# A two-part kernel on one core: PSUM banks taken oldest first in the projection stage, loop tiles laid over inputs, output weights loaded last from SyncE, twelve copies moved to ScalarE

## Chip, cores, metric

One core of one Trainium2 chip. The metric is the device time of one execution in microseconds (us), the median of several; lower is better. A single profiled execution of each kernel gives the traces; its span (first to last instruction) is about 1.8 us shorter than its time.

In this kernel TensorE writes its products to banks of the memory PSUM; VectorE or ScalarE copies them out to SBUF, from where TensorE reads its operands; SyncE and ScalarE issue the transfers (DMA) between SBUF and DRAM. In the profile lines, SPq and ACTq are such issues by SyncE and ScalarE, with the time that the issue itself took. A DMA share of 1.0 or a little above means that the 16 DMA engines were full.

## The reference, cut to what matters

`x` is 2048 x 512. The result is a gated mix of two attention branches over the same `x`.

```python
g = _sigmoid((x * gate_w).sum(-1, keepdims=True))
a = _A_ref(x, ...)      # 64 segments of 32 rows, 32 heads of 128; 8 memory rows go from segment to segment
b = _B_ref(x, ...)      # 32 heads of 16, 4 blocks of 512 rows; a state of phi(k) v goes from block to block
return g * a + (1 - g) * b

# in A, for each segment (strictly one after the other):
h = jnp.concatenate([mem, xs], axis=1)
q, k, v = h @ Wq, h @ Wk, h @ Wv        # 512 -> 32 x 128
p = _softmax(q k^T, masked)
o = jnp.einsum('bhte,hed->btd', p v, Wo)
mem = o[:, :M, :]                       # the next segment needs this
# in B: phi = lambda t: jnp.where(t > 0, t + 1.0, jnp.exp(t)), for keys and queries
```

The kernel runs B's projections (keys, queries, values, phi) first, as a **first stage** of some 70 us, and stores them to DRAM. Then the **loop** over A's 64 segments (13.3 us each) takes up B's attention beside it, reading those tensors back. While the first stage runs, A's weights (Wk, Wq, Wv, Wo, 4.19 MB each) are loaded.

## The kernel before: the parts concerned

```python
class Banks:                                  # the eight PSUM banks
    def take(self, long=False):
        f = self.free                         # in the order in which they were given back
        if long:
            c = [b for b in f if b < 2] or f
        else:                                 # spare the whole pairs, if there are few
            whole = [b for b in f if b > 1 and b ^ 1 in f]
            c = [b for b in f if b not in whole and b > 1] if len(whole) <= 4 else [b for b in f if b > 1]
            c = c or [b for b in f if b > 1] or f
        b = c[0]
        f.remove(b)
        return b

# two layouts of the same stretch of SBUF: one for the first stage, one for the loop
in_p = alloc(esP, ("wkB", ...), ("wqB", ...), ("phK", ...), ("MZ16", ...), ...          # inputs
      ("etmp", [128, 512], BF16, 5), ("stgp", [128, 512], BF16, 3), ("stgk", [128, 512], BF16, 4), ("stgq", [128, 512], BF16, 4),
      ("V17", [128, 4, HB, 17], BF16, 0), ("wvB", [128, C, DM], BF16, 0))               # stg*, V17: staging of the stores
esP.close()
v.x_sb = v.Wo_sb[:, 0:NTT, :]                 # x lies in the first half of Wo's memory
in_a = alloc(esA, ("xL", ...), ("LN_sb", ...), ("KTL", ..., 2), ("QTL", ..., 2), ("VL", ..., 2), ("KN_sb", ...), ("QN_sb", ...),
      ("KT_sb", ...), ("QT_sb", [128, H // 2, L, 2], BF16, 0), ("V_sb", ...), ...)      # QT_sb falls on stgp

# the first stage, piece by piece
for n in range(len(pieces)):
    ...                                       # x chunks, gates
    pieces[n]()                               # a projection, its copy out of PSUM, its store from SyncE
    if n in (50, 52, 54, 56):
        bat.load(0, n // 2 % 2, "kv"[n // 54])          # the first blocks of B read back
    if weights and n % 4 == 2 and n > 5:
        weights.pop(0)()                      # one load of 1 MB from ScalarE: Wk x4, Wq x4, Wv x4, Wo x4
while weights:
    weights.pop(0)()                          # the rest, and B's output weights
plan_a(v, NSEG_RUN)                           # the loop

# one quarter of Wo, from ScalarE's queue; a single semaphore group for all four
P.dma(grp, lambda s: s.dma_start(v.Wo_sb[:, 8 * q:8 * q + 8, :], wosrc[:, 8 * q:8 * q + 8, :]),
      writes=[Rs("Wo")] + [...], name="dma_Wo%d" % q, eng="act")

# copies out of PSUM in the first stage
v.evac("dve" if m == "k" else "act", stage[:, :], v.pb[bk], ...)                        # keys, queries
v.evac("act" if tt % 2 else "dve", v.V17[:, tt, :, 0:16], v.pb[bk]...)                  # values
```

The softmax here doesn't subtract the row's maximum and nothing guards it: scores larger than these inputs give would overflow.

## Time and profile before

| | before |
|---|---|
| time, median of 3 | 947.72 us (946.32 to 948.25) |
| span of the profiled run | 946.2 us |
| segment 1 of the loop begins (its first projection of `hT`) | 99.86 us |
| from there to the end | 846.3 us |

TensorE's timeline of the kernel before in the first stage (start, busy time, engine, line, operation, tiles, shapes, count, and in brackets the idle time before and what ended it):

```profile
13.46 0.81 PE L634 MATMUL ps<-xT,wqB 128*128 128x512 bf16 x3 [0.79 <-DVE stgk L357]
16.81 1.04 PE L634 MATMUL ps<-xT,wqB 128*128 128x512 bf16 x4 [0.56 <-DVE stgk L357]
...
28.39 0.81 PE L634 MATMUL ps<-xT,wqB 128*128 128x512 bf16 x3 [1.47 <-DVE xT L357]
```

A projection (in two of the twelve cases below a transpose) waits for the copy that empties the bank it is to write: the bank rule gives out one emptied a moment ago. There are twelve such waits from 10 to 60 us, 8.6 us together.

ScalarE's queue at the end of the stage, where Wo is issued:

```profile
64.76 0.39 ACTq L502 DMA_DIRECT2D Wo_sb<-in_A_Wo_dram  x1
68.27 0.41 ACTq L502 DMA_DIRECT2D Wo_sb<-in_A_Wo_dram  x1
70.91 4.01 ACTq L502 DMA_DIRECT2D Wo_sb<-in_A_Wo_dram  x2
```

The issue of one 1 MB load normally takes 0.4 us of the queue. The last pair takes 4.01 us: when its second issue began, at about 71.3 us, three loads were outstanding (the first of them landed at 73.7), and the queue held ScalarE up until 74.9. The last quarter of Wo landed at 87.5 us.

### The profile page before, as it was taken

Reading aid. Unit: us, or ns where it says so; the run is one execution under the profiler, and the core shown is the slowest. Engines: PE = TensorE matmul, PEld = TensorE weight load, DVE = VectorE, ACT = ScalarE, POOL = GpSimd, SP = SyncE. Lnnn points to the kernel's source line nnn. Section 1 sums busy time; section 2 is a strip of 40 time slices with the busy share of each in tenths; the row PEclk is TensorE's granted clock in tenths of the full one; section 3 lists DMA queues with packets and bytes.
Section 4 is the critical chain, followed back from the end, with each engine's and each line's share of the span. In section 5 each row is a group of like instructions: output and inputs, shape, how many; then the busy total and the mean of one; then the engine's idle time right before and its main releaser. Section 6 shows DMA issues by size and latency. Waiting matters only on the chain. (4 is left out here: it accounts for less than half of the span.)

```text
span 946.2 us, 51712 instructions
## 1 busy us (share of the span) xinstructions
PE 875.4 (93%) x23175; PEld 466.7 (49%) x23182; DVE 635.1 (67%) x1388; ACT 575.4 (61%) x1339; POOL 243.6 (26%) x553
## 2 busy tenths in 40 slices
PE   8886989999899999999999989999999999999885
PEld 3443545555454545555455545545455555544442
DVE  4763666676666786776776777667767677677564
ACT  3542666666666766666666665666666666664553
POOL 3610222222222231322222232222222232221110
PEclk9997999999999999999999999999999999999999
DMA  9997000000001121101001110100101110000110
GB/s 305 371 343 247 13 13 16 15 21 18 22 9 38 32 54 28 27 16 27 16 21 49 32 44 20 28 15 19 41 16 41 31 43 24 24 3 9 37 37 8
DMA packets 66052, 51.36 MB, mean 54 GB/s; under 512 B 34464, under 2 KB 64296, under 8 KB 64296
## 3 DMA queue, kind: packets, MB, share of 16 engines
q1 hardware_dynamic: 59944, 31.29, 12.1%
q10 hardware_dynamic: 5888, 16.78, 5.0%
q8 instruction: 182, 2.98, 1.3%
q14 instruction: 38, 0.31, 0.1%
HBM read 33.47 MB, written 14.57 MB: 51 GB/s over the span
## 5 line engine op out<-in xcount | busy, mean ns | idle before, releaser
L801 ACT ACTIVATE PT<-ps 128x1024 bf16<-128x1024 f32 x160 | 163.8, 1024 | 1.8
L947 PE MATMUL ps<-Wv_sb,hT 128*32 128x512 bf16 x2048 | 143.5, 385 | 0.0
L947 PE MATMUL ps<-Wq_sb,hT 128*32 128x512 bf16 x2048 | 134.5, 380 | 0.0
L947 PE MATMUL ps<-Wk_sb,hT 128*32 128x512 bf16 x2048 | 132.7, 379 | 0.0
L808 POOL TENSOR_SCALAR_AFFINE_SELECT PT<-PT 128x512 bf16<-128x512 bf16 (+1 forms) x96 | 75.8, 789 | 199.9 <-ACT PT L801 175.3
L1000 PE MATMUL ps<-Wo_sb,OT_sb 128*32 128x512 bf16 x2048 | 123.4, 380 | 0.3 <-DVE OT_sb L357 0.2
L357 DVE CAST V_sb<-ps 128x512 bf16<-128x512 f32 x128 | 88.5, 691 | 47.7 <-PE ps L947 47.7
L1218 POOL TENSOR_TENSOR P_sb<-P_sb,R_sb 128x64 bf16<-128x64 bf16 x128 | 47.4, 371 | 280.0 <-PE ps L1172 166.7
L959 DVE STREAM_TRANSPOSE QT_sb<-QN_sb 128x256 f32<-128x256 f32 x128 | 56.7, 443 | 77.9 <-ACT QN_sb L355 70.1
L355 ACT ACTIVATE QN_sb<-ps 128x512 bf16<-128x512 f32 x128 | 77.1, 602 | 31.3 <-PE ps L947 28.8
L355 ACT ACTIVATE OT_sb<-ps 128x320 bf16<-128x320 f32 x128 | 56.0, 437 | 61.9 <-PE ps L1241 59.7
L1011 DVE TENSOR_TENSOR WL<-ps,WH 128x256 bf16<-128x256 f32 x128 | 54.3, 424 | 46.0 <-ACT WH L355 42.5
L1181 ACT ACTIVATE P_sb<-ps 128x224 bf16<-128x224 f32 x128 | 45.2, 353 | 60.8 <-PE ps L1172 60.8
L947 PEld LDWEIGHTS ps<-Wk_sb,hT 128*32 128x32 bf16 x2048 | 54.0, 97 | 48.7 <-ACT KN_sb L355 1.2
L357 DVE CAST OT_sb<-ps 128x320 bf16<-128x320 f32 x128 | 61.8, 483 | 20.3 <-PE ps L1241 18.9
L947 PEld LDWEIGHTS ps<-Wq_sb,hT 128*32 128x32 bf16 x2048 | 49.7, 96 | 44.6 <-ACT hT L355 9.3
L959 DVE STREAM_TRANSPOSE KT_sb<-KN_sb 128x256 f32<-128x256 f32 x128 | 56.5, 441 | 21.3 <-ACT KN_sb L355 19.1
L1000 PEld LDWEIGHTS ps<-Wo_sb,OT_sb 128*32 128x32 bf16 x2048 | 48.1, 96 | 45.1 <-DVE OT_sb L357 5.5
L787 PE MATMUL ps<-QTj,KTj 32*128 32x256 bf16 (+1 forms) x768 | 62.9, 255 | 4.3 <-ACT PT L801 3.6
L355 ACT ACTIVATE WH<-ps 128x256 bf16<-128x256 f32 x64 | 24.6, 384 | 62.6 <-PE ps L1000 59.7
L1205 ACT ACTIVATE R_sb<-ps 128x160 f32<-128x160 f32 x128 | 39.1, 305 | 35.8 <-PE ps L1198 35.8
L1228 PE MATMUL ps<-P_sb,V_sb 32*128 32x40 bf16 x2048 | 36.3, 178 | 22.2 <-ACT OT_sb L355 7.7
(131 smaller groups left out, 1578.5 us busy)
## 6 DMA issues: line engine op xcount, KB each, us to landing
Wk_sb<-in_A_Wk_dram ACTq DMA_DIRECT2D x4, 1024.0 KB, 6.9
Wq_sb<-in_A_Wq_dram ACTq DMA_DIRECT2D x4, 1024.0 KB, 8.2
Wv_sb<-in_A_Wv_dram ACTq DMA_DIRECT2D x4, 1024.0 KB, 7.8
Wo_sb<-in_A_Wo_dram ACTq DMA_DIRECT2D x4, 1024.0 KB, 10.9
scr_vd<-V SPq DMA_DIRECT2D x16, 136.0 KB, 6.3
Vj<-scr_vd SPq DMA_DIRECT2D x32, 68.0 KB, 2.5
Wo_sb<-in_A_x_dram SPq DMA_DIRECT2D x8, 256.0 KB, 6.1
scr_kTd<-stgk SPq DMA_DIRECT2D x16, 128.0 KB, 8.0
```

Source lines behind the costliest of these rows:

```text
L355: P.op("act", lambda a: a.activation(dst, src, ACT.Copy), reads=[v.rbank[k] for k in bks], writes=dres, name=name)
L357: P.op("dve", lambda d: d.tensor_copy(dst, src), reads=[v.rbank[k] for k in bks], writes=dres, name=name)
L787: ins = pe.matmul(v.pb[bks[x]][:, 256 * e + o:256 * e + o + w], KT[e][r, 128 * kc:128 * (kc + 1)], QT[r, q0:q0 + w], start=True, stop=True ...
L801: P.op("act", lambda a: a.activation(pt[:, :, :], v.ps[:, bks[0]:bks[1] + 1, :], ACT.Exp, scale=v.SCALE_B), reads=[v.rbank[b] for b in bks ...
L808: P.op("gp", lambda g: g.affine_select(mv, mv, [[0, mv.shape[1]], [1, 128]], ALU.is_ge, 0.0, base=0, channel_multiplier=-1), reads=[rp], w ...
L947: ins = pe.matmul(pb[bk][SEG * j:SEG * (j + 1), :], lhs(c), cols(w, j) if split else w[:, 512 * j:512 * (j + 1)], start=(c == 0), stop=(c ...
L959: P.op("dve", lambda d: d.transpose(to, src), reads=reads, writes=writes, name=name)
L1000: ins = pe.matmul(pb[bk][SEG * j:SEG * (j + 1), :], lhs(4 * k + j), Wo_sb[:, 4 * k + j, :], start=(first and k == ks[0]), stop=False, skip ...
L1011: P.op("dve", lambda d: d.tensor_tensor(lo[:, c], pb[bk][:, c], hi[:, c], ALU.subtract), reads=[rbank[bk], Rs(res[0][hf])], writes=[Rs(res ...
L1181: P.op("act", lambda a: a.activation(P_sb[:, b, :], pb[bk][:, 0:224], ACT.Exp, scale=SCALE), reads=[rbank[bk]], writes=[Rs("P%d" % b), Rs( ...
L1205: P.op("act", lambda a: a.activation(R_sb[:, b, :], pb[bk][:, 224:384], ACT.Ln), reads=[rbank[bk]], writes=[Rs("R%d" % b)], name="ln%d_%d" ...
L1218: P.op(ENG["n"], lambda d: d.tensor_tensor(left(P_sb), left(P_sb), grp04(R_sb[:, b, :]), ALU.mult), reads=[Rs("R%d" % b)], writes=[Rs("P%d ...
```

## The change

The intent: TensorE shall not wait for banks in the first stage (oldest bank first; twelve copies from the busier VectorE to ScalarE). The loop's first tiles shall not wait for the last stores (they are laid over inputs, which engines have finished reading, not over staging buffers that stores still read). ScalarE's queue shall not be held up at the end of the stage (Wo is issued by SyncE after all stores; B's output weights only in segment 1). For that, the A weights start earlier (n = 2, not 6), and so do the first blocks read back (n = 36 to 42, not 50 to 56).

The tile lists are cut to their names here.

```diff
 class Banks:
+        self.oldest = True
...
+        elif self.oldest:
+            c = [b for b in f if b > 1] or f
...
-    in_p = alloc(... wkB, wqB, phK, MZ16, bmask, mem0_sb, gwr_sb, beta_sb, gB_sb, omgB_sb, etmp x5, stgp x3, stgk x4, stgq x4, V17, wvB)
+    in_p = alloc(... wkB, wqB, phK, etmp x5, bmask, mem0_sb, gwr_sb, beta_sb, gB_sb, omgB_sb, wvB, MZ16, stgk x4, stgq x4, V17, stgp x3)
-    in_a = alloc(... xL, LN_sb, KTL x2, QTL x2, VL x2, KN_sb, QN_sb, KT_sb, QT_sb, ...)
+    in_a = alloc(... xL, LN_sb, KTL0, QTL0, VL0, KN_sb, QN_sb, KT_sb, QT_sb, ..., KTL1, QTL1, VL1, ...)
...
-        if n in (50, 52, 54, 56):
-            bat.load(0, n // 2 % 2, "kv"[n // 54])
-        if weights and n % 4 == 2 and n > 5:
+        if n in (36, 38, 40, 42):
+            bat.load(0, n // 2 % 2, "kv"[n // 40])
+        if weights and n % 4 == 2:
             weights.pop(0)()
-    while weights:
-        weights.pop(0)()
+    v.wo_load()                                   # the four Wo loads, one after the other, from SyncE
+    v.BK.oldest = False
+    v.BK.free = sorted(v.BK.free)
     plan_a(v, NSEG_RUN)
...
-        v.evac("dve" if m == "k" else "act", stage[:, :], ...)
+        v.evac("dve" if m == "k" and f < 3 else "act", stage[:, :], ...)
-        v.evac("act" if tt % 2 else "dve", v.V17[:, tt, :, 0:16], ...)
+        v.evac("act", v.V17[:, tt, :, 0:16], ...)
...
+        if s == 1:
+            v.wob_load()                          # B's output weights, in segment 1
```

More of the change, by code (lines that the diff above doesn't have):

```diff
@@ L282, in build @@
     esP = ExitStack()
-    in_p = alloc(esP, ("wkB", [128, C, DM], BF16, 0), ("wqB", [128, C, DM], BF16, 0), ("phK", [128, 4, DM], BF16, 0), ("MZ16", [128, 544], BF16, 0),
+    in_p = alloc(esP, ("wkB", [128, C, DM], BF16, 0), ("wqB", [128, C, DM], BF16, 0), ("phK", [128, 4, DM], BF16, 0), ("etmp", [128, 512], BF16, 5),
           ("bmask", [128, 136], BF16, 0), ("mem0_sb", [128, DM], BF16, 0), ("gwr_sb", [128, 128], BF16, 0), ("beta_sb", [128, HB], BF16, 0),
-          ("gB_sb", [128, HB], F32, 0), ("omgB_sb", [128, HB], F32, 0),
-          ("etmp", [128, 512], BF16, 5), ("stgp", [128, 512], BF16, 3), ("stgk", [128, 512], BF16, 4), ("stgq", [128, 512], BF16, 4),
-          ("V17", [128, 4, HB, 17], BF16, 0), ("wvB", [128, C, DM], BF16, 0))
+          ("gB_sb", [128, HB], F32, 0), ("omgB_sb", [128, HB], F32, 0), ("wvB", [128, C, DM], BF16, 0), ("MZ16", [128, 544], BF16, 0),
+          ("stgk", [128, 512], BF16, 4), ("stgq", [128, 512], BF16, 4), ("V17", [128, 4, HB, 17], BF16, 0), ("stgp", [128, 512], BF16, 3))
     esP.close()
@@ L291, in build @@
     esA = ExitStack()
-    in_a = alloc(esA, ("xL", [128, C, SEG], BF16, 0), ("LN_sb", [128, 2, 512], BF16, 0), ("KTL", [128, H // 2, SEG, 2], BF16, 2), ("QTL", [128, H // 2, SEG, 2], BF16, 2),
-          ("VL", [128, 2, 512], BF16, 2), ("KN_sb", [128, 2, 512], BF16, 0), ("QN_sb", [128, 2, 512], BF16, 0),
-          ("KT_sb", [128, H // 2, SEG, 2], BF16, 0), ("QT_sb", [128, H // 2, L, 2], BF16, 0), ("V_sb", [128, 2, 512], BF16, 0),
-          ("P_sb", [128, 2, 224], BF16, 0), ("R_sb", [128, 2, 160], F32, 0),
-          ("OT_sb", [128, H, L], BF16, 0), ("OTL", [128, H, SEG], BF16, 2),
+    LT = [128, H // 2, SEG, 2]
+    in_a = alloc(esA, ("xL", [128, C, SEG], BF16, 0), ("LN_sb", [128, 2, 512], BF16, 0), ("KTL0", LT, BF16, 0), ("QTL0", LT, BF16, 0), ("VL0", [128, 2, 512], BF16, 0),
+          ("KN_sb", [128, 2, 512], BF16, 0), ("QN_sb", [128, 2, 512], BF16, 0), ("KT_sb", LT, BF16, 0), ("QT_sb", [128, H // 2, L, 2], BF16, 0),
+          ("V_sb", [128, 2, 512], BF16, 0), ("P_sb", [128, 2, 224], BF16, 0), ("R_sb", [128, 2, 160], F32, 0),
+          ("OT_sb", [128, H, L], BF16, 0), ("OTL", [128, H, SEG], BF16, 2), ("KTL1", LT, BF16, 0), ("QTL1", LT, BF16, 0), ("VL1", [128, 2, 512], BF16, 0),
           ("oTt", [128, 16, 32], F32, 0), ("t1_sb", [128, DM], F32, 0), ("aT_st", [128, C, 128], BF16, 2))
+    v.KTL, v.QTL, v.VL = [v.KTL0, v.KTL1], [v.QTL0, v.QTL1], [v.VL0, v.VL1]
     esA.close()
@@ L499, in plan_loads, with wo @@
     wosrc = v.A_Wo.rearrange("h e d -> e h d")
-    for q in range(4):
-        def wo(q=q):
-            P.dma(grp, lambda s: s.dma_start(v.Wo_sb[:, 8 * q:8 * q + 8, :], wosrc[:, 8 * q:8 * q + 8, :]),
-                  writes=[Rs("Wo")] + ([Rs("x_sb%d%d" % (k, h)) for k in (2 * q, 2 * q + 1) for h in range(2)] if q < 2 else []), name="dma_Wo%d" % q, eng="act")
-        pend.append(wo)
+    def wo():
+        for q in range(4):
+            P.dma(grp, lambda s, q=q: s.dma_start(v.Wo_sb[:, 8 * q:8 * q + 8, :], wosrc[:, 8 * q:8 * q + 8, :]),
+                  writes=[Rs("Wo")] + ([Rs("x_sb%d%d" % (k, h)) for k in (2 * q, 2 * q + 1) for h in range(2)] if q < 2 else []), name="dma_Wo%d" % q)
+    v.wo_load = wo
     def wob():
@@ L512, in wob @@
                 P.dma(grp, lambda s, j=j, g=g, o=o: s.dma_start(v.woB_sb[o:o + 16, :, :], rows[g, j]), writes=[Rs("woB")], name="dma_woB%d%d" % (j, g))
-    pend.append(wob)
+    v.wob_load = wob
     return pend
@@ L621, in rest @@
         def rest():
-            P.op(eng, lambda d: d.tensor_scalar(et, et, 1.0, None, op0=ALU.min), reads=[re], writes=[re], name=name + "_m")
+            P.op("dve", lambda d: d.tensor_scalar(et, et, 1.0, None, op0=ALU.min), reads=[re], writes=[re], name=name + "_m")
             P.op(eng, lambda d: d.scalar_tensor_tensor(dst, src, 0.0, et, ALU.max, ALU.add), reads=[rsrc, re], writes=wres, name=name)
@@ L639, in pk @@
         rs = Rs("stg%s%d" % (m, i % 4))
-        v.evac("dve" if m == "k" else "act", stage[:, :], v.pb[bk], [bk], [rs], "ev%s%d_%d" % (m, sb, f))
+        v.evac("dve" if m == "k" and f < 3 else "act", stage[:, :], v.pb[bk], [bk], [rs], "ev%s%d_%d" % (m, sb, f))
         store("st%s%d_%d" % (m, sb, f), dram[sb, f], stage[:, :], [rs], [Rs("%sTd%d_%d" % (m, sb, f))], "st%s%d_%d" % (m, sb, f),
@@ L661, in pv @@
         rv = Rs("V17_%d" % tt)
-        v.evac("act" if tt % 2 else "dve", v.V17[:, tt, :, 0:16], v.pb[bk].rearrange("p (h d) -> p h d", d=16), [bk], [rv], "evv%d_%d" % (sb, tt))
+        v.evac("act", v.V17[:, tt, :, 0:16], v.pb[bk].rearrange("p (h d) -> p h d", d=16), [bk], [rv], "evv%d_%d" % (sb, tt))
         store("stv%d" % sb, v.vd[sb, :, tt, :], v.V17[:, tt, :, :].rearrange("p h w -> p (h w)"), [rv, Rs("V17o")], [Rs("vd%d_%d" % (sb, tt))],
```

## The prediction

> **What bounds the kernel now.** I read the page first. In its 40 slices (about 24 us each) the TensorE row stands at 9 from the sixth slice on, and the DMA engines are full only in the first four slices and nearly idle after. So there are two regimes: a loop of about 850 us bound by TensorE, and a first stage of about 100 us in which DMA is saturated. The chain of work that ended last reaches back only to 629 us, so it says nothing of the first stage.
>
> ```profile
> PE   8886989999899999999999989999999999999885
> PEclk9997999999999999999999999999999999999999
> DMA  9997000000001121101001110100101110000110
> ```
>
> The change touches only the first stage and how the loop is entered. I built both kernels and compared instruction order: TensorE and GpSimd execute the same instructions in the same order, and in the loop the waits of every TensorE instruction are the same in both. Bank numbers differ only by a renaming, except at six hand-overs right where the loop begins. The loop should therefore cost what it costs now, and the question is when it gets going.
>
> Next, the busy time per stretch of 10 us (columns: TensorE, weight load, VectorE, ScalarE, GpSimd; granted clock; DMA share; GB/s).
>
> ```profile
> 10.00:20.00 10.00, 8.08 (x61) 4.50 (x61) 7.41 (x16) 5.54 (x11) 2.09 (x10) 1.00 1.01 330
> ...
> 60.00:70.00 10.00, 8.91 (x53) 4.60 (x54) 7.76 (x15) 5.51 (x9) 0.36 (x1) 1.00 0.98 318
> 70.00:80.00 10.00, 9.14 (x157) 4.18 (x158) 4.68 (x9) 3.52 (x7) 0.30 (x1) 1.00 1.06 341
> 80.00:90.00 10.00, 3.14 (x75) 1.42 (x68) 2.12 (x5) 0.92 (x3) 0.67 (x2) 0.68 0.83 280
> 90.00:100.00 10.00, 10.00 (x236) 4.73 (x232) 6.00 (x13) 5.51 (x14) 2.47 (x6) 0.80 0.02 4
> ```
>
> Three things: the DMA share is 1.0 from 10 to about 88 us and then drops to nothing; TensorE is idle some 7 us between 80 and 90; and its clock falls because of that. The timelines say why.
>
> ```profile
> 79.20 0.62 SPq L610 DMA_DIRECT2D scr_pQd<-stgp  x1
> 86.65 0.45 DVE L959 STREAM_TRANSPOSE QT_sb<-QN_sb 128x256 f32<-128x256 f32 x1 [7.53 <-DMA scr_pQd<-stgp]
> 87.52 0.38 PE L1165 MATMUL ps<-mneg,ident 128*32 128x224 bf16 x4 [6.86 <-POOL hT L1124]
> 95.89 0.83 PE L1000 MATMUL ps<-Wo_sb,OT_sb 128*32 128x512 bf16 x12
> 99.86 1.05 PE L947 MATMUL ps<-Wq_sb,hT 128*32 128x512 bf16 x16
> ```
>
> The loop's QT_sb lies in memory where the staging buffers stgp lay. The last phi(q) store left SyncE's queue at 79.20 us and landed 7.4 us later; VectorE's first transpose waited 7.53 us for it, and scores and TensorE waited behind that (6.86 us). "POOL hT" is only the last of the semaphores; GpSimd waited for the same store. The first use of the output weights Wo is at 95.89 us, and segment 1 starts at 99.86 us.
>
> **What the Trainium skill says.** "TensorE: Matmul & The Clock Gate", Part 1: after an idle window of about 3.4 us the clock halves, and it needs about 3.4 us of sustained work to recover. The trace agrees on the first half: in stretches of 2 us the granted clock is 0.92 at 82, 0.50 from 84 to 92, 0.52 at 92 and 1.00 at 94. Recovery took about 6.5 us from 87.5, so up to two windows.
>
> "DMA: Bandwidth & Descriptors", Specifications: the HBM limit for one core is about 358 GB/s. The seven full stretches above run at 318 to 380, so the first stage sits on that limit. The same page ("Queues, rings and completion order") says that SyncE's and ScalarE's queues are rings on the same 16 engines. No trace here contradicts that; hence issuing Wo from SyncE adds no bandwidth.
>
> **The change, part by part.**
>
> *Banks oldest first.* TensorE is busy 8.08+8.48+8.26+7.90+8.51+8.91 = 50.1 of the 60 us from 10 to 70, so 9.9 us are idle. Matching the idle pieces of the timeline to the banks, eight or nine pieces of 0.4 to 1.5 us are waits for a bank emptied just before (0.79 at 13.46, 0.56 at 16.81, 0.57 at 19.50, 1.47 at 28.39, three of 0.56, 1.01 at 45.05, and so on): about 8 us. The new rule hands out the bank that was freed longest ago, some five banks back.
>
> *Copies moved to ScalarE.* Twelve copies (8 values, 4 keys) leave VectorE at 0.69 us: -8.3 us; ScalarE gains 12 x 0.60 = 7.2 us. From 10 to 70 VectorE falls from 42.7 to about 34.5 and ScalarE rises from 31.2 to about 38. Both stay below TensorE's 50, so neither becomes the bound. Taken alone, these two parts would bring the first stage's end on TensorE (70.80 us now) to about 62.
>
> *DMA caps that.* Bytes from the issue rows: weights A 12.58 MB, Wo 4.19, x 2.10, B's three weights 1.57, stores of k, q, phi(q), v and the state 8.42, first loads 0.39, the B output weights 0.52: 29.8 MB. They go from about 2 to 88 us, 346 GB/s. The stage cannot outrun its stores by more than its staging (15 buffers, 2 MB). (29.8 - 4.19 - 0.52 - 2.0) / 0.346 + 2 = 69 us if all A weights are ahead of them; a few MB of weights may still be in flight, so I take 65 to 69 for the end of the stage.
>
> *Loop tiles over inputs.* QT_sb and the others now lie over the B weights and etmp, whose last readers are engine instructions of the first stage. In the built kernel no store is left in the waits of segment 0's transposes, softmax or values; the stores that remain (keys 0 and 1, the state) are early ones. The 7.53 us wait, and TensorE's 6.86, go away.
>
> *Wo last, from SyncE; B output weights after it.* ScalarE loses a queue stall (one Wo issue held it for 3.6 us at 71.3). Wo landed at 71.3 + 16.2 = 87.5 us. Now only the 0.52 MB of B output weights step behind it, worth 1.5 us: **Wo lands at about 86 us**, since everything ahead of it still has to pass the same full engines. All of Wo is waited for at once.
>
> *The sum.* Left-over projections take 70.80 to 77.03 now, 5.3 without the 0.86 us wait inside. An undisturbed segment goes from its first projection to its first Wo product in 9.13 us (139.16 to 148.29). TensorE would ask for Wo at 67 + 5.3 + 9.1 = 81, and wait for it until 86. From there segment 1 starts 3.97 us later (95.89 to 99.86 now): 90 against 99.86, a gain of 9.9 us. A wait of about 5 us may halve the clock again: the 32 Wo products and what follows then cost 1 to 2.5 us more. I take 1.2: a gain of 8.7, and **939.0 us**.
>
> **The rivals.**
> 1. *Compute sets the end.* Were Wo there in time, segment 1 would start at 62 + 5.3 + 9.1 + 4.0 = 80.4: a gain of 19 us, to about 928. For it: the bank waits are real. Against it: 29.3 MB by 76 us is 395 GB/s, above every 10 us stretch here. Very unlikely whole; a better DMA rate could give a part, to 935.
> 2. *The Wo wait is longer or colder.* SyncE issues Wo only after its last store; if stores are late (weights now start earlier and crowd them, so VectorE waits for stgp as it did for 7.2 us in all), the engines may run dry before Wo starts, or one queue alone may move less (272 to 281 GB/s from 2 to 6 us, with only SyncE's queue). Wo then lands at 88 to 90 with a cold clock: 942 to 944.
> 3. *The first stage does not shorten,* because crowded stores stop it. Then TensorE asks for Wo at 70.8 + 14.4 = 85, finds it nearly there, and the clock stays up: 938. That is nearly the same time by another road, and why I trust the sum.
> 4. *The loop changes* with renamed banks or moved tiles. The waits are the same; I allow 1 us either way.
>
> **Range and chances.** Wo's landing, 84 to 88.5 us, gives -2 to +2.5; the clock -1.2 to +1.5; run-to-run spread 1: together 935.5 to 943. Faster by over 2% needs under 928.8, i.e. rival 1 whole: 0.03. Slower by over 2% has no mechanism here: 0.01. Within 2%: 0.96.
>
> **What would show it.** Right: VectorE's wait for the phi(q) store before QT_sb is gone; TensorE's longest wait of the first 100 us is before a Wo product and ends with the Wo load, at 84 to 88 us; the DMA share is 1.0 until then; the idle time from 10 to 60 us shrinks; segment 1 starts at 89 to 93; from there to the end it takes 846 us as now. Wrong: Wo landed before TensorE asked for it (rival 1), a DMA share well below 1 between 60 and 85 (rival 2), or a loop that is longer or shorter by over 2 us (rival 4).

## More of the kernel before

Line numbers in profiles of the changed kernel are about five higher than here.

## The result and the profile after

**942.88 us** (median of 4: 939.45, 942.8, 942.97, 943.49), against 947.62 of the kernel before (median of 4). The ratio is 0.9944, 95% interval 0.9918 to 0.997. Ratios here are the mean time of one kernel's fast runs over that of the other's of the same rounds, so not quite the ratio of the medians quoted. The predicted 939.0 is 3.9 us too low. The measured median lies just inside the range, at its slow end; a second series of the unchanged kernel (below) gave 944.23, just outside it. A gain of 8.7 us was forecast and one of 3.4 to 4.7 came.

The profiled run was the fastest of the four (span 937.7). Its stretches, from 10 us on (columns: from:to, length, busy time of TensorE, weight load, VectorE, ScalarE and GpSimd, granted clock, DMA share, GB/s):

```profile
10.00:20.00 10.00, 9.95 (x70) 5.51 (x71) 6.71 (x15) 7.58 (x15) 2.14 (x10) 1.00 1.05 388
20.00:30.00 10.00, 8.99 (x69) 5.05 (x70) 5.36 (x11) 6.28 (x12) 6.58 (x26) 1.00 1.05 415
30.00:40.00 10.00, 6.74 (x47) 3.53 (x48) 5.02 (x12) 6.05 (x12) 6.85 (x23) 1.00 1.04 409
...
60.00:70.00 10.00, 9.69 (x105) 4.31 (x107) 6.99 (x14) 6.76 (x13) 0.54 (x1) 1.00 0.82 273
70.00:80.00 10.00, 8.48 (x227) 4.45 (x218) 5.51 (x12) 5.32 (x12) 2.23 (x6) 1.00 0.94 296
80.00:90.00 10.00, 5.25 (x105) 2.24 (x109) 2.47 (x5) 1.36 (x3) 1.07 (x3) 0.54 0.83 227
```

TensorE is now nearly always busy at first, the stage moves bytes faster (409 to 415 GB/s), and TensorE reaches the end of the stage at 65.79 us, not 70.80. But from 60 us the DMA share falls to 0.82, at a time when 4.19 MB of Wo are still to come. Between 80 and 90 TensorE is idle for 4.75 us and its clock is near half (0.54; 0.68 before).

TensorE's waits in the first stage, in the same view as before:

```profile
27.75 0.40 PE L679 MATMUL ps<-ident,stgk 128*128 128x128 bf16 x4 [0.78 <-DVE stgk L360]
36.90 0.81 PE L663 MATMUL ps<-wvB,xT 128*128 128x512 bf16 x3 [1.92 <-ACT V L358]
40.46 1.04 PE L639 MATMUL ps<-xT,wqB 128*128 128x512 bf16 x4 [1.77 <-DVE phK L628]
```

These are all that are left from 10 to 60 us, 4.5 us instead of 8.6. The second is new: ScalarE's copy into V17 itself waited 3.4 us for the store of the values before to read that buffer. The third stands behind VectorE, which had just waited 4.8 us for a phi(q) store. The stage runs into its stores.

The entry into the loop, on VectorE and on TensorE:

```profile
72.70 0.45 DVE L964 STREAM_TRANSPOSE QT_sb<-QN_sb 128x256 f32<-128x256 f32 x1 [0.80 <-ACT QN_sb L358]
```

```profile
80.44 0.39 PE L952 MATMUL ps<-Wk_sb,xL 128*32 128x512 bf16 x1 [1.96 <-issue]
87.62 3.60 PE L1005 MATMUL ps<-Wo_sb,OT_sb 128*32 128x512 bf16 x32 [4.31 <-DMA Wo_sb<-in_A_Wo_dram]
93.31 1.05 PE L952 MATMUL ps<-Wq_sb,hT 128*32 128x512 bf16 x16
```

The 7.53 us wait for the phi(q) store is gone. In its place TensorE waits 4.31 us for Wo, and then runs the 32 Wo products at half clock (3.60 us; 1.91 at full clock). Segment 1 starts at 93.31, a gain of 6.55 us, and the rest takes 844.4 us, 1.95 us less than before. This last part is not the change's doing as far as the record shows: in the traces below the same loop takes 844.4 to 847.5 us, with no pattern that follows the edits.

Why Wo is late stands in SyncE's queue and in the chain of waits:

```profile
67.34 0.44 SPq L615 DMA_DIRECT2D scr_qTd<-stgq  x1
67.83 0.47 SPq L615 DMA_DIRECT2D scr_vd<-V  x1
68.34 0.47 SPq L615 DMA_DIRECT2D scr_pQd<-stgp  x1
68.86 2.10 SPq L615 DMA_DIRECT2D scr_vd<-V  x3
71.00 6.23 SPq L507 DMA_DIRECT2D Wo_sb<-in_A_Wo_dram  x4
```

```profile
74.44 13.04 DMA Wo_sb<-in_A_Wo_dram
```

From 59.08 to 71.00 SyncE issues 22 stores of 128 to 136 KB, one after the other with hardly a gap, 0.54 us each. That pace is some 248 GB/s (2.96 MB in 11.92 us): the DMA engines get no more than SyncE hands them. They were not behind: the stores issued from 66 to 69 us landed after 1.9 to 3.7 us (medians by tensor), most of those from 50 to 60 us after 5.1 to 7.4 us. SyncE is behind its producers: the phi(q) store issued at 68.34 was ready at 66.5. Wo, which waits for nobody, stands behind all of them in the same queue. Its last quarter is issued at 74.44 and lands 13.04 us later, at 87.49. That is the moment at which it landed before the change.

An estimate of what was lost, from the trace: from 62 to 74 us the engines moved 242 GB/s on average. In the best experiment below they moved 377 in that time. The difference over 12 us is 1.6 MB; from 74 to 84 us they moved 356 GB/s, so it costs 4.5 us. Wo would have landed at 83.0, and TensorE asked for it at 87.62 - 4.31 = 83.3.

### The profile page after: what moved, and what is told of

Read it like the earlier page. It is cut to its first block, busy times and chain, and to the rows that moved or that the text cites. A ratio compares the mean times of both kernels' runs of the same rounds, so it can differ in the third digit from the quotient of the medians.

```text
span 937.7 us, 51704 instructions
## 1 busy us (share of the span) xinstructions
PE 874.1 (93%) x23175; PEld 465.8 (50%) x23182; DVE 626.8 (67%) x1376; ACT 580.9 (62%) x1351; POOL 243.8 (26%) x553
## 4 chain that ended last, share of the span: by engine, by line
PE 83%; ACT 5%; DVE 5%; DMA 4%; issue 2%; SPq 0%; ACTq 0%; DVEq 0%
PE ps L952 44%; PE ps L1005 15%; PE ps L792 5%; PE ps L1233 3%; PE ps L1027 2%; DMA scr_pQd<-stgp 2%; ACT PT L806 2%; PE ps L1177 2%; PE ps L639 2%; DVE WL L1016 2%; PE ps L1203 1%; PE ps L839 1%; DMA Wo_sb<-in_A_Wo_dram 1%; PE ps L1170 1%; PE ps L1246 1%
## 5 line engine op out<-in xcount | busy, mean ns | idle before, releaser
L1005 PE MATMUL ps<-Wo_sb,OT_sb 128*32 128x512 bf16 x2048 | 125.3, 384 | 4.5 <-DMA Wo_sb<-in_A_Wo_dram 4.3
```

Source lines behind the costliest of these rows:

```text
L1005: ins = pe.matmul(pb[bk][SEG * j:SEG * (j + 1), :], lhs(4 * k + j), Wo_sb[:, 4 * k + j, :], start=(first and k == ks[0]), stop=False, skip ...
```

## The experiments

Twelve runs on two chips: eight on one; on another the second run with Wo on ScalarE, the one with Wo early from SyncE, the one with both edits, and the one with the copies back. Each kernel was timed in five rounds beside the kernel before (947.4 to 947.6 us). All results were correct. By the 2% rule all twelve are "the same" as the kernel before; what follows compares ratios to it, with their 95% intervals. The edits are against the changed kernel unless said otherwise.

### The changed kernel again

> The changed kernel again, beside which the others of this job are to be read, and to see why its four runs so far spread (939.45, then 942.8 to 943.5). Theory: the span is set by when Wo lands (87.5 us in the profile at hand) and by how long the clock stays at half after the wait; I expect 942 to 943 as the middle of the runs, Wo landing at 86 to 90 us and segment 1 starting 5.5 to 7 us after. Rival: the spread comes from the loop; then Wo and segment 1 stand where they stood and the loop (844.4 us from segment 1 to the end in the profile at hand) is some 3 us longer.

No edit. 944.23 us (941.63 to 947.99), ratio 0.9964 [0.9944, 0.9984]. In this run's trace TensorE waited longer for Wo:

```profile
91.17 3.60 PE L1005 MATMUL ps<-Wo_sb,OT_sb 128*32 128x512 bf16 x32 [6.13 <-DMA Wo_sb<-in_A_Wo_dram]
```

Wo's last quarter was issued at 76.84 and landed at 91.04, so 3.55 us later than in the first trace; the span is 942.2, 4.5 us longer. So between these two traces most of the difference is Wo's landing. For the other executions there is no trace.

### Wo back on ScalarE, spread over the end of the stage

```diff
-    v.wo_load()
+    # the four Wo loads are in the list of weights again: n = 50, 54, 58, 62, from ScalarE (eng="act")
```

> The changed kernel, but Wo issued from ScalarE's queue right behind the other weights (about 54 to 64 us), as the kernel before did, in place of last from SyncE. Theory (Wo last from SyncE leaves the DMA engines underfed from 62 to 74 us, because SyncE issues one 128 KB store per 0.45 us and Wo waits behind them all): the DMA share stays at 1.0 until Wo has landed, Wo lands at 81 to 84 us, the wait before the first Wo product is under 1.5 us, segment 1 starts at 86 to 89, and the time falls by 4 to 6 us against the control. Rival (Wo last is what lets the stores through, and issuing it from ScalarE blocks that queue): first stage ends at 69 us or later, ScalarE shows an issue of over 2 us, time equal to the control or up to 3 us above it.

938.83 us (935.17 to 941.82), ratio 0.9907 [0.9886, 0.9928]; in the same session the changed kernel had 0.9964, and the intervals don't meet. Stretches, then TensorE:

```profile
60.00:70.00 10.00, 8.49 (x62) 3.41 (x60) 3.88 (x8) 5.42 (x11) 0.29 (x1) 1.00 1.09 372
70.00:80.00 10.00, 9.65 (x176) 4.58 (x177) 6.13 (x13) 4.13 (x8) 0.96 (x3) 0.83 1.09 369
80.00:90.00 10.00, 10.00 (x272) 5.02 (x268) 6.96 (x15) 6.56 (x16) 2.32 (x6) 1.00 0.10 27
```

```profile
84.85 1.91 PE L1005 MATMUL ps<-Wo_sb,OT_sb 128*32 128x512 bf16 x32
```

The DMA engines stay full until about 81 us and are then done. Wo is there when asked for, and the clock is up. There is a price: the stores now share the engines with Wo, VectorE's waits for stgp rise from 9.0 to 16.2 us, and the first stage's end moves back (segment 0's first projection at 75.50; 70.98 and 73.13 in the two traces of the changed kernel): that much of the rival came true. No issue on ScalarE took over 0.42 us. Segment 1 still starts at 88.83. The profiled execution is the fastest of its six (935.17), so this trace flatters the kernel.

### The same kernel again, on another chip

> The kernel with Wo from ScalarE at n = 50 to 62, once more, as the partner of the run before it on the same chip and to see whether its 938.8 (ratio 0.9907) holds. Theory: 937.5 to 940.5, ratio 0.989 to 0.993, no wait before the first Wo product, clock 1.00. Rival (the first result was luck): over 941.

939.8 us (937.84 to 942.0), ratio 0.9913 [0.9894, 0.9932]. The profiled run was a slower one (941.11), with segment 1 at 93.36: the stage stood longer behind its stores (segment 0 from 79.78), but no Wo product waited, and all of them ran at full clock. The gain holds.

### Wo in the same places, but from SyncE

```diff
-              ..., name="dma_Wo%d" % q, eng="act")
+              ..., name="dma_Wo%d" % q)           # SyncE; places n = 50, 54, 58, 62 as in the run above
```

> The changed kernel with the four Wo loads at the places in the first stage where the kernel with Wo on ScalarE had them (n = 50, 54, 58, 62), but from SyncE. It tells the place in time from the queue. If the place is what matters (theory: the engines ran under-full from 62 us on because nothing large was outstanding beside SyncE's stores), the DMA engines are full from 50 to 80 us (share above 1.0, over 365 GB/s), TensorE finds Wo there at its first Wo product, and the time is 937 to 941, as with Wo on ScalarE. If the queue is what matters (rival: SyncE's one queue carries less, or a 1 MB load ahead of the stores in it holds the phi(q) stores and so VectorE's wait for stgp), the stage ends later on TensorE, stgp waits sum to over 18 us, and the time is 942 to 945.

940.56 us (938.46 to 942.48), ratio 0.9918 [0.9901, 0.9935], next to 0.9913 for ScalarE on the same chip. The changed kernel itself was not timed on this chip; its nearest partner there is the run with the copies back (0.9958 [0.9942, 0.9973]), whose interval meets neither. So in time the **place** decides; a difference between the queues can't be measured. The trace is between the two theories. SyncE works in order and is late, so the same four places come at 63.35 to 77.08 us instead of 52.85 to 68.34 (56.34 to 72.04 in the second run on ScalarE):

```profile
63.35 0.45 SPq L507 DMA_DIRECT2D Wo_sb<-in_A_Wo_dram  x1
...
77.08 0.89 SPq L507 DMA_DIRECT2D Wo_sb<-in_A_Wo_dram  x1
```

From 64 to 76 us the engines moved 324 GB/s (253 in the changed kernel, 381 with ScalarE). TensorE still waited 2.88 us for Wo, on a cold clock:

```profile
87.86 3.60 PE L1005 MATMUL ps<-Wo_sb,OT_sb 128*32 128x512 bf16 x32 [2.88 <-DMA Wo_sb<-in_A_Wo_dram]
```

My forecasts of no wait and of full engines failed (share 0.92 from 60 to 70 us). The last quarter was even issued later than in the first trace of the changed kernel (77.08; 74.44) and landed at the same time (87.72; 87.49): what the edit moved clearly forward is the first two (63.35 and 67.23; none before 71.00 there). VectorE's waits for stgp were 18.1 us, as the rival said, without its effect on the time.

### One semaphore for each quarter of Wo

```diff
-                  writes=[Rs("Wo")] + ...
+                  writes=[Rs("Wo%d" % q)] + ...           # a group of its own for each quarter
-        P.op("pe", f, reads=reads + [Rs("Wo")], ...)
+        P.op("pe", f, reads=reads + [Rs("Wo%d" % q) for q in sorted({k // 2 for k in ks})], ...)
```

> The changed kernel with one semaphore for each quarter of Wo in place of one for all; each product waits for its own quarter. Same loads, same queue, same order. Theory (TensorE's 4.3 us wait is for the landing of the last quarter only): the first Wo product starts within 0.5 us of being asked for, at about 83.5 us, the last quarter at about 87.5, no idle stretch above 2 us between them, segment 1 starts about 2 us earlier than in the control, time 1.5 to 3 us less. Rival (the wait is only put down to Wo, and the chain behind it needs the same time): time within 0.5 us of the control.

941.84 us (940.93 to 943.55), ratio 0.9939 [0.9924, 0.9955]: 2.4 us under the changed kernel by the medians, but the intervals overlap. The waits are now one for each late quarter:

```profile
86.16 0.61 PE L1004 MATMUL ps<-Wo_sb,OT_sb 128*32 128x512 bf16 x8 [1.78 <-DMA Wo_sb<-in_A_Wo_dram]
90.51 1.05 PE L1004 MATMUL ps<-Wo_sb,OT_sb 128*32 128x512 bf16 x8 [3.73 <-DMA Wo_sb<-in_A_Wo_dram]
```

TensorE begins with Wo at 83.34, but the last quarter still sets the end of the products. The split hides the work in between, not the landing. I had forecast no idle stretch above 2 us; the second is 3.73. After it the clock stayed at half until 98 us.

### Both: Wo from ScalarE and a semaphore for each quarter

The two edits together.

> Wo from ScalarE at n = 50 to 62, and one semaphore for each quarter of Wo. Theory: Wo is all there when TensorE asks for it, so single semaphores for the quarters release nothing earlier: within 1 us of the run with one semaphore (937.5 to 940.5). Rival: part of Wo still lands last in some executions, so the quarters save up to 2 us: 936 to 937.5.

939.91 us (939.22 to 941.26), ratio 0.9914 [0.9899, 0.993], the same as with one semaphore. Where Wo is early, there is nothing left for the split to release.

### The old memory layout in the changed kernel

```diff
     in_p = alloc(...)    # both lists as in the kernel before; all else as changed
     in_a = alloc(...)
```

> The changed kernel with the old memory layout: loop tiles over the staging buffers of the stores again. Prediction's step: the layout takes away a wait of 7.5 us. Theory now (with Wo and the loads out of their way the last stores land at about 70 to 72 us, before or just when the loop's first transposes are ready at 72.7, and Wo at 87.5 sets the pace anyway): QT_sb waits for a store for less than 2 us, Wo lands where it did, time within 1 us of the control. Rival (the layout is where the gain came from): VectorE waits 5 us or more for the last phi(q) or key store, first Wo product later than 90 us, time back at 946 to 948.

943.77 us (942.77 to 944.65), ratio 0.9958 [0.9943, 0.9973]: the changed kernel's own time. QT_sb lies over stgp again, but waited for no store:

```profile
73.21 0.45 DVE L964 STREAM_TRANSPOSE QT_sb<-QN_sb 128x256 f32<-128x256 f32 x1 [0.80 <-ACT QN_sb L358]
```

With no Wo beside them, the last stores land before QT_sb needs their memory. TensorE then waited 6.77 us for Wo, which landed at 90.3. Within the whole change the new layout is worth nothing that can be measured.

### The new layout alone, in the kernel before

```diff
 # against the kernel before
-    in_p, in_a = ...     # old lists
+    in_p, in_a = ...     # new lists; nothing else changed
```

> The kernel before with the new memory layout and nothing else of the change. Theory (in the kernel before the layout's wait of 7.5 us is real and on the path; behind it stands Wo, landed at 87.5 us): the wait of QT_sb for a store is gone, TensorE asks for Wo at about 87 and waits less than 2 us, the clock stays up, segment 1 starts at 91 to 93 in place of 99.9, time 939 to 942, so as good alone as the whole change. Rival (layout worthless here too, as in the changed kernel): 946 to 948.

940.81 us (940.11 to 944.07), ratio 0.9938 [0.992, 0.9956]. VectorE, and TensorE at the first Wo product:

```profile
79.94 0.42 DVE L959 STREAM_TRANSPOSE QT_sb<-QN_sb 128x256 f32<-128x256 f32 x1
```

```profile
89.95 1.91 PE L1000 MATMUL ps<-Wo_sb,OT_sb 128*32 128x512 bf16 x32 [0.59 <-ACT OT_sb L355]
```

The store's wait is gone, and hardly a Wo wait comes in its place: Wo is issued at the places of the kernel before, here at 66.0 to 72.5 us. It is just in time: the last quarter landed at 89.8, so the 0.59 us may be a wait for it, though the profile names a copy (with Wo early on ScalarE the first Wo product starts before that copy does). The clock is 1.00 in every stretch from 60 us on, and segment 1 starts at 93.93. This one part gives as much as the whole change (0.9944 and 0.9964; the intervals overlap).

### The old layout with Wo from ScalarE

```diff
 # against the kernel with Wo on ScalarE at n = 50 to 62
     in_p, in_a = ...     # old lists
```

> Wo from ScalarE's queue from 53 us on, with the old memory layout. Theory (the layout is worth nothing only where the last stores have the engines to themselves; with Wo's traffic beside them they land late again): the last phi(q) store lands at 78 to 81 us, VectorE waits 1.5 to 5 us for it before QT_sb, and the time is 2 to 5 us above the 938.8 of the same kernel with the new layout. Rival (the layout never mattered): within 1 us of 938.8.

941.8 us (940.53 to 943.47), ratio 0.994 [0.9925, 0.9954], 2 to 3 us over the same kernel with the new layout (0.9907 and 0.9913; the intervals just overlap). Here the old layout has its wait again, though a short one:

```profile
81.33 0.45 DVE L964 STREAM_TRANSPOSE QT_sb<-QN_sb 128x256 f32<-128x256 f32 x1 [1.97 <-DMA scr_pQd<-stgp]
```

So the layout pays where the last stores land late: about 6 us in the kernel before, 2 to 3 here if it is more than noise, nothing measurable where Wo is last.

### Wo from ScalarE, but late

```diff
 # against the kernel with Wo on ScalarE and split semaphores
-        if weights and n % 4 == 2:
+        if weights and (n % 4 == 2 if n < 48 else n % 2 and n > 56):     # Wo at 64.0 to 68.1 us
```

> Wo from ScalarE's queue again, but in the last pieces of the first stage (about 60 to 66 us, after the other weights have landed), and with one semaphore per quarter. Theory: stores of the first three quarters of the stage keep their share, so the first stage ends on TensorE at about 65 to 66 and the loop starts 2 to 3 us earlier than with Wo from 53 us on (75.5 there); DMA share near 1.0 until Wo has landed at 82 to 85; no wait over 1.5 us for Wo; 934 to 938, that is at or below the 938.8 of Wo from 53 us on. Rival (four issues close together block ScalarE's queue for 3 us or more, as one did in the kernel before): the copies of the left-over projections wait, the loop starts later, 939 to 942.

940.75 us (939.79 to 942.85), ratio 0.9929 [0.9912, 0.9945]; about 2 us over the earlier places, with intervals that overlap. My forecast (934 to 938) failed and the rival came true. ScalarE's queue stands still, as the change's intent feared:

```profile
68.10 5.00 ACTq L506 DMA_DIRECT2D Wo_sb<-in_A_Wo_dram  x1
73.21 0.60 ACT L358 ACTIVATE LN_sb<-ps 128x512 bf16<-128x512 f32 x1 [4.52 <-PE ps L951]
```

The copy that ScalarE does next starts right when the issue ends. The cost of putting large loads on an engine that also has work is thus real, but here it came only when they were issued close together: at 52.85, 60.36, 65.29 and 68.34 us no issue took over 0.42 us.

### The old bank rule in the changed kernel

```diff
-        self.oldest = True
+        self.oldest = False
```

> The changed kernel with the first stage's banks handed out by the rule of the kernel before; all else as changed. Theory (Wo's landing sets when the loop starts, and Wo is issued behind SyncE's row of stores from about 60 to 73 us, which the banks hardly move): TensorE is idle 4 to 8 us more between 10 and 60 us, asks for Wo later, but finds it landed at 88 to 92 us as before; time within 2 us of 944. Rival (the banks are where the gain over the kernel before came from): 947 or more.

945.19 us (941.26 to 947.59), ratio 0.9971 [0.9948, 0.9995]; the changed kernel had 0.9964 on the same chip. The bank waits are back (0.79 at 13.54, 1.43 at 28.24, twelve of them with 8.6 us up to 60), and segment 0 starts at 75.67, not 73.13. TensorE then waits 1.59 us for Wo instead of 6.13, because Wo landed at 89.28. So what the bank rule saves is spent waiting for Wo. In this pair of traces segment 1 even starts 2.7 us earlier with the old rule (94.68; 97.39), and the loop takes 2.7 us longer (847.5; 844.8); why the loop differs is not known.

### The twelve copies back on VectorE

```diff
-        v.evac("dve" if m == "k" and f < 3 else "act", ...)
+        v.evac("dve" if m == "k" else "act", ...)
-        v.evac("act", v.V17[...], ...)
+        v.evac("act" if tt % 2 else "dve", v.V17[...], ...)
```

> The changed kernel with the twelve PSUM copies back on VectorE. Theory: VectorE is not the bound of the first stage and Wo's landing sets the start of segment 1, so the time is that of the changed kernel itself, 942.5 to 945. Rival: VectorE, which waits for stgp and then has a row of work to make up, is the path of the stage: its busy time rises by some 8 us, the stage ends 2 to 4 us later on TensorE, the last stores and Wo follow, and the time is 946 to 948.

943.75 us (943.22 to 945.99), ratio 0.9958 [0.9942, 0.9973]: no difference that can be measured from the changed kernel (0.9964, timed on the other chip). VectorE is busy 35.7 us of the 50 from 10 to 60, so not the bound, and TensorE waited 5.96 us for Wo.

### The entry into the loop, in nine of the profiled runs

Start times in us; segment 0 and segment 1 stand for their first projection of `hT`.

| kernel | segment 0 | first wait for Wo, us | its Wo products from | segment 1 | from there to the end |
|---|---|---|---|---|---|
| before | 77.03 | none | 95.89 | 99.86 | 846.3 |
| changed | 70.98 | 4.31 | 87.62 | 93.31 | 844.4 |
| changed, again | 73.13 | 6.13 | 91.17 | 97.39 | 844.8 |
| old layout | 71.49 | 6.77 | 90.45 | 96.31 | 845.7 |
| old banks | 75.67 | 1.59 | 89.42 | 94.68 | 847.5 |
| Wo early, SyncE | 72.17 | 2.88 | 87.86 | 94.14 | 844.6 |
| Wo early, ScalarE | 75.50 | none | 84.85 | 88.83 | 844.7 |
| Wo early, ScalarE, again | 79.78 | none | 89.38 | 93.36 | 846.0 |
| layout alone | 78.11 | none | 89.95 | 93.93 | 845.0 |

The last column stays within 3.1 us, and does not follow the edits. But 3 us is as much as some of the effects argued here, so single traces rank these kernels only roughly. The column of waits shows the trap: where segment 0 starts earliest, the wait for Wo is long.

**The best kernel** is the changed one with Wo from ScalarE at n = 50 to 62: 938.83 and 939.8 us, 0.9% under the kernel before and, on the same chip, 0.6% under the changed one.

## Why the prediction was right or wrong

The parts, in the prediction's order:

- *Banks and copies.* The stage's end was put at 65 to 69 us; it came at 65.79. But only 3.8 us of idle time came back in 10 to 60 us (8.77 to 4.94), not 8: waits for stores came up beside the bank waits. That the end still fell into the range is in part luck, since the rate it was computed from was too low (see "DMA caps that" below). The cause "banks" holds (the old rule brings the same waits back). The copies give nothing that can be measured.
- *Loop tiles over inputs.* The wait of 7.53 us did go. Alone, this part is worth about 6 us (layout alone). Within the changed kernel it would have gone anyway (old layout, no store wait), since Wo last leaves the stores the engines to themselves. I added it to the sum as if it stood by itself.
- *"DMA caps that", 346 GB/s.* The constant was too low: stretches of 409 and 415 GB/s in the trace after. I used the skill's limit of 358 GB/s, cited in the prediction, and the average before. My own table should have warned me: of the "seven full stretches" three ran at 375 to 380, above that limit. Had Wo been issued in time, this would have been a gain, as rival 1 allowed in part: the engines were done at 81 us with Wo early on ScalarE.
- ***"Wo lands at about 86 us", the step that failed.*** Its reason was that "everything ahead of it still has to pass the same full engines". They were not full. From 62 to 74 us they ran at a share of 0.77 and 242 GB/s, because all that was outstanding came from SyncE, one store per 0.54 us, and Wo stood in line behind. The Trainium skill names this case: "Perfetto Trace Analysis", What "DMA-bound" means, lists the sequencer of the issuing engine, with a track of solid DMA slices, as a bound apart from the DMA engines. SyncE's row from 59 to 71 us is that picture. I had rightly seen that another queue adds no bandwidth, and didn't ask whether one queue at that point could hand out enough. Wo landed at 87.49 in the fast profiled run and at 91.04 in the control, 1.5 to 5 us late. It was rival 2 that came true; I had given it as 942 to 944.
- *The clock.* Taken as 1.2 us. From the first Wo product to segment 1 it took 5.69 us, against 3.97 in an undisturbed entry: 1.7 us, and 2.3 in the control (6.22). Before Wo TensorE lost more: it needed 12.33 us from segment 0 to its request, not 9.13. Of that, 1.96 us is a stall named "issue", after which the clock already stood at 0.50 from 81 us. This part did not set the time, since TensorE then waited for Wo anyway.
- *The loop* took 844.4 to 844.8 us, 1.5 to 1.95 less than in the one trace of before: just inside the 2 us that I had set as the sign of rival 4. Traces with the same loop differ by more, so the record doesn't show that the change made it shorter.

In the sum: request at 83.3 (predicted 81), Wo at 87.5 to 91.0 (86), segment 1 at 93.3 to 97.4 (91.2). That the profiled execution took 939.45, almost the predicted 939.0, is luck: segment 1 came 2.1 us late, and the loop was 1.95 us shorter than assumed.

Shown, by undoing and by adding: the place of the Wo loads is what costs the changed kernel 3 to 5 us (two runs early on ScalarE, one early on SyncE); the layout, the bank rule and the copies are each worth nothing measurable beside Wo last; the layout is worth about 6 us in the kernel before. That SyncE's pace of issuing is what kept the engines under-full is read from the trace and fits the run with Wo early from SyncE; it was not isolated (see below).

**Open.** TensorE's "issue" stalls of 1.3 to 3.5 us at 80 to 87 us are in nearly every run in which the DMA engines were still full then, and missing or 0.2 us in the three with Wo early on ScalarE and the new layout. In the kernel before, TensorE was waiting for the store at that time. What TensorE lacks there the trace doesn't tell. The stalls stand at the same place of the program each time, in segment 0's first products of Wk_sb with xL, and the profile's table of DMA queues has some of kind "instruction" on the same engines; whether TensorE waited for its instructions was not tested. Nor is it settled whether the new layout alone (0.9938) is really slower than Wo early with everything else (0.9907, 0.9913): the intervals just meet or overlap. Three things were not run: the last stores shared between SyncE's and ScalarE's queues, which would part SyncE's pace from what stores to DRAM can take; the bank rule and the copies where Wo is early; and the earlier start of the A weights and of B's first blocks by itself.

## What to carry to other kernels

Gains at one hand-over don't add: after the first wait is gone, the next one is set by whatever lands last, and two cures of the same wait count once. A large load that waits for nothing should be outstanding early, between small stores, so that the DMA engines never depend on one queue's pace of issuing; issued last, it begins only when the issuer has worked off its backlog. Spread such loads out if they come from an engine that has work, because here the fourth in a row held its queue for 3 to 5 us.

## What the Trainium skill lacked or had wrong

- "DMA: Bandwidth & Descriptors", Issuing engines are not separate DMA queues: it calls the sequencer time saved by issuing from several engines usually small beside the transfer. Here, as the trace reads, it was the bound: 22 stores of 128 to 136 KB took SyncE 0.54 us each, and kept the engines at 242 GB/s for 12 us (377 with 1 MB loads beside them).
- No page says how much a queue takes before it holds up the engine that issues ("Perfetto Trace Analysis" mentions only a descriptor buffer that can fill up): the fourth 1 MB load issued close behind three others held ScalarE's queue for 5.00 us, and a pair took 4.01 us in the kernel before.
- "DMA: Bandwidth & Descriptors", Specifications: the row of about 358 GB/s for a core does not say that it is no cap for a core that runs alone; mixed loads and stores moved 409 and 415 GB/s over stretches of 10 us. This is easy to misread rather than wrong: the page's section on Bandwidth gives 425 for one large load on a single core, and I should have used that.
- "TensorE: Matmul & The Clock Gate", Part 1: recovery after about 3.4 us of work is the lower end. Counted from the first product after the wait it took about 3.5 us in the changed kernel's trace, 5 in the control, 6.4 before, and about 8 with the split semaphores.
